# A two-part mixing network behind a linear recurrence: the whole first half in one written order, the token product on three column parts of the array, values and states stored head by head

## The chip, the cores and the metric

The kernel runs on one core of one Trainium2 chip. The metric is the device time of one execution in microseconds (us). The engines are TensorE (PE, with its weight loads PEld), VectorE (DVE), ScalarE (ACT), GpSimd (POOL) and SyncE (SP), whose queue issues nearly all transfers.

## What is computed

Four batches, eight heads, 768 positions, head size 48, so 384 channels. All arrays are float32 to the reference, but the weights arrive in a wider format and are unpacked on the chip.

```python
for t in range(S):                       # gated complex recurrence per head
    S_re, S_im = (ar*S_re - ai*S_im + k v^T, ar*S_im + ai*S_re)
    y[t] = q[t] . S_re
x = y as (batch, position, channel)
# first mixture
h = x^T @ U @ V                          # rank 32, over the positions
u = x + h^T
x = u + relu(u @ w_ch1) @ w_ch2          # 384 -> 1536 -> 384
# second mixture
theta = x @ w_theta
zr, zi = x*cos(theta), x*sin(theta)
u = x + w_tok_r @ zr + w_tok_i @ zi      # 768 x 768 over the positions
out = u + relu(u @ w_ch)
```

## The kernel before

**Attention.** The recurrence is computed in 24 chunks of 128 positions (six to a batch). Two chunks make a pair: `load` brings its four rows, `ew` does some 30 elementwise operations on 128 x 768 elements on VectorE and ScalarE (square roots, an arctangent, two running scans, sine and cosine), and `gather` moves the results into `QK`, one 96 x 258 block a head, with five transfers for each half of it. Then `pe_steps` does a chunk on TensorE: `score` (line 453, 8 products of 128 columns), `mask` and `select` (ScalarE copies the scores out, GpSimd zeroes the upper triangle), `ktr` (line 469, 8 transposes of k) and `kn_` (ScalarE copies them out), `xst` (line 492, 8 products for the new state), `add` (VectorE), `yt` (line 521, the output, two heads side by side on two 64-column halves of the array), `ycp`, `ytr` (line 535, transposed back) and a copy into `xs`. The values `vt` and states `a_st` are stored in pairs of heads with 48 zeros between the two, so that a product can take 96 or 64 columns from a head with zeros at the right place. `gx` (line 546) adds the chunk's share of x^T U with U repeated three times (96 columns of weights, 384 moving columns).

**First mixture.** `g_steps` splits x^T U into a high and a low part and multiplies by V (`hx`, line 576). `mlp_steps` then goes through three blocks of 256 positions a batch, each in six units: `f_unit` (line 711, 18 matmuls of 256 columns; ScalarE and VectorE copy the result out as `rh` and `rl`) and `c_unit` (line 736, 12 matmuls of 384 columns). `prologue` transposes x (line 682) for each block.

**Weights.** `unpack` turns each wide weight into a high and a low part with one load, one or two ScalarE and five VectorE operations: 22 jobs for the first mixture and U, V in the first phase, 16 for the second mixture, whose results partly go out to `tokd` in DRAM.

**What sets the order.** `startup` lists the steps of the first two batches' attention, of the jobs for the first mixture and of batch 0's `mlp_steps`. `ranks` gives each a rank (its longest path to the end, shifted by the table `LEAD`), `schedule` walks through time with a cost for every step (`COST`, `HOP`) and places the ready step with the lowest rank. `fixed` issues the steps in that order and ties VectorE, ScalarE and GpSimd to it (`HELD`). TensorE and the transfers are not tied; neither is anything of batches 2 and 3 (`attention`), of `mains` for batches 1 to 3 and of the 16 later jobs. Those are ordered by the compiler's list scheduler from the priorities of the lanes (`a2`, `a3`, `w3`, `moe`, `evac`).

**Second mixture.** `front` (projection, sine and cosine) and `mix` (the 768 x 768 product, line 971, and the channel product, line 987) run after that, ordered by the list scheduler.

Of the kernel before, what the change touches and what calls it, by code (L numbers as in the profile page):

```python
# [56 lines left out]
PLANNED = 2  # L57
# [30 lines left out]
def schedule(steps, rank, bias, hop=HOP, window=400):  # L88
# [20 lines left out]
    while ready:  # L109
        cand, low = [], 1e18  # L110
        for n in ready:
# [3 lines left out]
            if new:  # L115
                free = [x for x in frees[new[0][0]] if x is not None]
                if not free:
# [27 lines left out]
        at[e], end[n] = en, en + hop[e]  # L145
# [14 lines left out]

def ranks(steps, names, lead, hop=HOP):
# [4 lines left out]
    for n, nm in enumerate(names):  # L166
        if nm == "m0":
# [10 lines left out]
    for n, nm in enumerate(names):  # L178
        k = cnt[nm] = cnt.get(nm, -1) + 1
        r0, dr = lead.get(nm, (0, 0))  # L180
# [8 lines left out]
def attn_moe_kernel(tc, pk, qn, kn, v, are, aim, U, V, w1, w2, wth, wtr, wti, wch, out):  # L189
# [14 lines left out]
    ctx = ExitStack()  # L204
    const = ctx.enter_context(tc.tile_pool(name="const", bufs=1))
# [10 lines left out]
    stg = [xf[:, PLANNED * NC * C + i * 1536:PLANNED * NC * C + (i + 1) * 1536] for i in range(3)]  # L216
# [29 lines left out]
    vt_fs = [ac.tile([128, NP * 3 * D + 16], F32, name=f"vt{i}") for i in range(2)]  # L246
    vts = [t[:, 0:NP * 3 * D].rearrange("p (r z e) -> p r z e", z=3, e=D) for t in vt_fs]
    for t in vt_fs:
        G_.memset(t, 0.0)
    carry = ac.tile([128, NJ, 1], F32, name="carry")  # L250
    a_fs = [ac.tile([96, NP * 3 * D + 16], F32, name=f"a_st{i}") for i in range(2)]
    a_sts = [t[:, 0:NP * 3 * D].rearrange("p (r z e) -> p r z e", z=3, e=D) for t in a_fs]
    for t in a_fs:
        G_.memset(t, 0.0)
# [6 lines left out]
    wa = wp.tile([128, KF * C], F32, tag="w", name="wa")  # L261
    wb = wp.tile([128, KF * C], F32, tag="w", name="wb")
    e_store = dict(key="E", lo=er[:, 0:5], hi=er[:, 5:])

    w_store = dict(key="W", **{n: t[:, 0:5 * NR].rearrange("p (z n) -> p z n", z=5) for n, t in (("lo", wa), ("hi", wb))})
# [935 lines left out]
```

## Time and profile before

| | us |
|---|---|
| median of 3 runs | 877.26 (877.17 to 877.9) |
| the profiled execution | 877.16 |
| its span, first to last instruction | 875.4 |
| busy: PE / DVE / ACT / POOL | 757.8 / 524.9 / 453.3 / 124.3 |
| first matmul of the first mixture (line 711) | starts at 142.0 |
| last attention output leaves, last `hx` | about 495 |
| first matmul of the second token product (line 971) | starts at 642.4 |

The profile is read from the top: the slices tell where TensorE is full and at which granted clock, the windows give the busy time of each engine in a stretch, the waits name who held whom, and the chain of waits tells which of these ended last.

### The profile page before, as it was taken

How to read it: one execution, taken by the hardware profiler on the slowest of the kernel's cores; microseconds unless marked ns; L12 is line 12 of the kernel's file. 1: busy time of each engine (PE TensorE's matmuls, PEld its weight loads, DVE VectorE, ACT ScalarE, POOL GpSimd, SP SyncE). 2: the span in 40 equal slices, each digit the busy share in tenths (PEclk: the TensorE clock that was granted, in tenths of full speed). 3: DMA queues.
4: the chain of work that ended last, by engine and by line, in shares of the span. 5: the costliest groups of instructions: out<-in, count | busy, mean ns of one | idle time of the engine just before them, and what ended most of it. 6: DMA issues, size and time to landing. Idle time of an engine off the chain costs nothing.

```text
span 875.4 us, 13800 instructions
## 1 busy us (share of the span) xinstructions
PE 757.8 (87%) x5338; PEld 717.1 (82%) x5338; DVE 524.9 (60%) x787; ACT 453.3 (52%) x772; POOL 124.3 (14%) x144
## 2 busy tenths in 40 slices
PE   0085588798989698989999999899999999999996
PEld 0075367686978698979999999899999999999996
DVE  6958988978819578668151587893244335253321
ACT  6965876757726976784433253444155345253300
POOL 1011010200000002010101000000064234133200
PEclk9995867999998799999999999999999999999999
DMA  9264463552332443540331137620060000000001
GB/s 259 75 177 122 115 184 82 161 165 75 91 91 55 118 119 82 128 113 19 95 87 27 55 128 266 212 99 1 1 218 1 28 28 27 1 28 28 28 28 31
DMA packets 105657, 79.78 MB, mean 91 GB/s; under 512 B 32912, under 2 KB 97424, under 8 KB 105584
## 3 DMA queue, kind: packets, MB, share of 16 engines
q1 hardware_dynamic: 105184, 78.62, 32.2%
q8 instruction: 44, 0.72, 0.3%
q10 hardware_dynamic: 400, 0.20, 0.1%
q14 instruction: 29, 0.24, 0.1%
HBM read 50.33 MB, written 9.44 MB: 68 GB/s over the span
## 4 chain that ended last, share of the span: by engine, by line
PE 59%; DVE 15%; ACT 10%; DMA 8%; issue 3%; SPq 3%; POOL 0%; DVEq 0%; ACTq 0%; POOLq 0%
PE h L711 10%; PE c L736 9%; PE h L971 9%; PE c L971 9%; PE m L920 4%; PE m L987 4%; DVE er L337 4%; PE m L453 4%; PE m L521 4%; DMA er<-in_pk_dram 2%; ACT er L334 2%; DVE er L340 2%; PE m L492 2%; DMA tok1l<-tl 2%; ACT L334 2%
## 5 line engine op out<-in xcount | busy, mean ns | idle before, releaser
L711 PE MATMUL h<-uh,w1h 128*128 128x256 f32 x432 | 126.8, 294 | 3.1 <-DVE rl L721 2.1
L711 PE MATMUL h<-ul,w1h 128*128 128x256 f32 x432 | 125.0, 289 | 1.4 <-DVE ul L692 1.4
L711 PE MATMUL h<-uh,w1l 128*128 128x256 f32 x432 | 124.3, 288 | 0.0
L463 POOL TENSOR_SCALAR_AFFINE_SELECT pt<-pt 128x512 f32<-128x512 f32 x48 | 45.8, 962 | 425.7 <-ACT pt L459 411.2
L337 DVE TENSOR_TENSOR er<-er 128x768 f32<-128x768 f32 (+1 forms) x99 | 101.9, 1054 | 4.0 <-ACT er L334 2.0
L736 PE MATMUL c<-w2h,rl 128*128 128x384 f32 x288 | 100.1, 348 | 4.1 <-DVE rl L721 4.0
L736 PE MATMUL c<-w2h,rh 128*128 128x384 f32 x288 | 95.6, 349 | 6.7 <-ACT rh L716 3.0
L736 PE MATMUL c<-w2l,rh 128*128 128x384 f32 x288 | 97.8, 342 | 1.2 <-DVE w2l L311 1.1
L721 DVE SCALAR_TENSOR_TENSOR rl<-h,rh 128x512 fp32r<-128x512 f32 x72 | 49.3, 685 | 78.8 <-ACT rh L716 78.8
L711 PEld LDWEIGHTS h<-uh,w1h 128*128 128x128 f32 x432 | 83.5, 193 | 6.1 <-DVE rl L721 2.7
L711 PEld LDWEIGHTS h<-ul,w1h 128*128 128x128 f32 x432 | 83.6, 193 | 1.9 <-DVE ul L692 1.6
L711 PEld LDWEIGHTS h<-uh,w1l 128*128 128x128 f32 x432 | 83.5, 193 | 0.4 <-issue 0.2
L334 ACT ACTIVATE er<-er 128x768 f32<-128x768 f32 x88 | 74.0, 845 | 16.0 <-DVE er L337 12.4
L716 ACT ACTIVATE rh<-h 128x512 fp32r<-128x512 f32 x72 | 42.8, 596 | 67.4 <-PE h L711 59.5
L453 PE MATMUL m<-QK 96*128 96x128 f32 x384 | 60.0, 303 | 10.9 <-DMA QK<-wa 8.8
L453 PEld LDWEIGHTS m<-QK 96*128 96x128 f32 x384 | 53.5, 211 | 15.3 <-issue 10.5
L340 DVE SCALAR_TENSOR_TENSOR er<-er 128x768 f32<-128x768 f32 x55 | 52.8, 966 | 20.2 <-ACT er L334 11.6
L469 PE MATMUL m<-ident,QK 96*128 96x96 f32 x160 | 22.8, 261 | 46.0 <-DMA QK<-er 44.3
L736 PEld LDWEIGHTS c<-w2h,rh 128*128 128x128 f32 x288 | 52.8, 190 | 9.5 <-ACT rh L716 3.9
L736 PEld LDWEIGHTS c<-w2h,rl 128*128 128x128 f32 x288 | 54.6, 190 | 6.5 <-DVE rl L721 6.0
L469 PEld LDWEIGHTS m<-ident,QK 96*128 96x128 f32 x160 | 18.2, 150 | 49.6 <-issue 48.6
L736 PEld LDWEIGHTS c<-w2l,rh 128*128 128x128 f32 x288 | 54.3, 189 | 2.3 <-DVE w2l L311 1.8
(209 smaller groups left out, 1741.3 us busy)
## 6 DMA issues: line engine op xcount, KB each, us to landing
er<-in_pk_dram SPq DMA_DIRECT2D x88, 192.0 KB, 3.7
QK<-er SPq DMA_DIRECT2D x88, 145.1 KB, 3.4
x<-in_moe_w_ch_dram SPq DMA_DIRECT2D x9, 512.0 KB, 4.4
vt<-in_v_dram SPq DMA_DIRECT2D x48, 96.0 KB, 2.7
x<-in_moe_w_ch_dram SPq DMA_DIRECT2D x12, 384.0 KB, 3.4
st<-in_moe_w_tok_i_dram SPq DMA_DIRECT2D x6, 768.0 KB, 5.6
st<-in_moe_w_tok_r_dram SPq DMA_DIRECT2D x6, 768.0 KB, 4.2
out_dram<-x SPq DMA_DIRECT2D x23, 192.0 KB, 2.3
```

The source lines that it names most:

```text
L334: do("A", size, r, w, lambda e: A_.activation(out=out, in_=in_, func=func, **kw), tab)
L337: do("V", size, r, w, lambda e: V_.tensor_tensor(out=out, in0=in0, in1=in1, op=op))
L340: do("V", size, r, w, lambda e: V_.scalar_tensor_tensor(out=out, in0=in0, scalar=scalar, in1=in1, op0=op0, op1=op1))
L453: PE.matmul(ps[:, hh * T:(hh + 1) * T], lhsT=st["QK"][:, h, 1, 0:T], rhs=st["QK"][:, h, 0, 0:T], start=True, stop=True)
L463: G_.affine_select(out=pt, in_=pt, pattern=[[0, 4], [1, T]], compare_op=ALU.is_ge, fill=0.0, base=0, channel_multiplier=-1)
L469: PE.transpose(ps[:, hh * 96:(hh + 1) * 96], st["QK"][:, 4 * i + hh, 1, 0:T], ident[0:96, 0:96])
L521: PE.matmul(st["y"][64 * z:64 * z + 64, r * T:(r + 1) * T], lhsT=wide(old_w if k else vt_w, h), rhs=st["QK"][:, h, 0, 0:T] if k else st[f" ...
L711: PE.matmul(ps[:, f, :], lhsT=a[:, k, fs], rhs=u[:, k, :], start=(k == 0 and i == 0), stop=(k == NJ - 1 and i == 2))
L716: A_.activation(out=rh, in_=rts[n, p], func=AF.Relu)
L721: V_.scalar_tensor_tensor(out=rl, in0=ps, scalar=0.0, in1=r32(rh), op0=ALU.max, op1=ALU.subtract)
L736: PE.matmul(chs[n, t][:, 0:C], lhsT=r[:, f, t * T:(t + 1) * T], rhs=w[:, k, :], start=(k == 0 and i == 0), stop=(k == KF - 1 and i == 2))
L971: PE.matmul(ps[k][:, 0:C], lhsT=z[:, 2 * part + o, k * 128:(k + 1) * 128], rhs=w[:, s, ts], start=(s == 0 and part == 0 and j == 0), stop= ...
```

## The change

- `PLANNED` goes from 2 to 4: attention of all four batches and all four `mlp_steps` become steps of the plan, and so do the final flags, the reopening of the memory for the second mixture and its 16 weight jobs (`reopen`, `later`, `mix2_jobs`). `HELD` now ties TensorE and SyncE too. `attention` and `mains` go. Keys `fo` and `co` keep the units of all batches in one sequence; the table `LEAD` is new throughout.
- `gx` of batches 1 to 3 uses U once (32 columns) in three products of 128 moving columns on three 32-column parts of the array. The result lies in three blocks of 32 partitions, so `down` copies it out and `side` sends it through DRAM and back, three transfers each way.
- `vt` and `a_st` hold the heads one behind another without zeros. `xst` has 48 moving columns instead of 96; `yt` takes 64 columns, of which 16 belong to the next head and are not read later. The values need one transfer a chunk instead of two.
- `n2` (a rounding of 128 x 768 elements) may go to VectorE as well as ScalarE.

```diff
-    'l0': (17.6, 55.3), 'e0': (1.2, 0.1), 'p0': (-49.1, -22.6), 'u': (-11.1, 38.3), 'x0': (283.2, 62.0),
+    'l0': (-560.6, 1239.0), 'e0': (-3421.5, 1361.7), 'p0': (-1222.3, -173.9), 'u': (1269.9, -523.9),
...
-PLANNED = 2
+PLANNED = 4
...
-                    d = (1.05 if tab else 1.25) * size
+                    d = (1.05 if tab else 1.1) * size
...
-        at[e], end[n] = en, en + hop[e]
+        at[e], end[n] = en, en + (steps[n][5] if e == "D" and steps[n][5] else hop[e])
...
-    vt_fs = [ac.tile([128, NP * 3 * D + 16], F32, name=f"vt{i}") for i in range(2)]
+    vt_fs = [ac.tile([128, C + 16], F32, name=f"vt{i}") for i in range(2)]
...
-            for z in range(2):
-                nc.sync.dma_start(out=vt[:, :, 2 * z, :], in_=v[b, z::2, c * T:(c + 1) * T, :].rearrange("r s e -> s r e"))
+            nc.sync.dma_start(out=vt, in_=v[b, :, c * T:(c + 1) * T, :].rearrange("h s e -> s h e"))
...
-        act(AF.Identity, n2, Bt, bias=b_magic, r=K("B"), w=K("n"), size=N + 100)
+        do(EL, (N + 100) / 2, K("B"), K("n"), lambda e: V_.tensor_scalar(
+            out=n2, in0=Bt, scalar1=MAGIC, scalar2=None, op0=ALU.add) if e == "V" else
+            A_.activation(out=n2, in_=Bt, func=AF.Identity, bias=b_magic))
...
-                for r in range(NP):
-                    for z in range(2):
-                        h = 2 * r + z
-                        PE.matmul(ps[0:96, r * 96:(r + 1) * 96], lhsT=st["kn"][:, h, :],
-                                  rhs=vw(h), start=(z == 0), stop=(z == 1))
+                for h in range(H):
+                    PE.matmul(ps[0:96, h * D:(h + 1) * D], lhsT=st["kn"][:, h, :], rhs=vt_w[:, h * D:(h + 1) * D],
+                              start=True, stop=True)
...
+                for j in range(NJ):
+                    PE.matmul(gps["ps"][j * R:(j + 1) * R, 0:128], lhsT=u4[:, c, 0:R], rhs=xs[b][:, c, j * 128:(j + 1) * 128],
+                              start=(c == 0), stop=(c == NC - 1))
...
+        def down(e):
+            gps["t"] = t = ap.tile([128, H * 2 * D], F32, tag="kn", name="gt")
+            A_.copy(out=t[0:NJ * R, 0:128], in_=gps["ps"][0:NJ * R, 0:128])
+
+        def side(e):
+
+            t = gps["t"]
+            gps["ps"] = t[:, 128:128 + C]
+            gd = gdp.tile([R, NJ, 128], F32, tag="gd", name="gd")
+            for j in range(NJ):
+                nc.sync.dma_start(out=gd[:, j, :], in_=t[j * R:(j + 1) * R, 0:128])
+            for y in range(3):
+                nc.sync.dma_start(out=gps["ps"][y * R:(y + 1) * R, :], in_=gd.rearrange("r j c -> r (j c)"))
...
-    HELD = ('DVE', 'Activation', 'Pool')
+    HELD = ('DVE', 'Activation', 'Pool', 'PE', 'SP')
...
-        ops = mlp_steps(0)
-        steps.extend(ops)
-        names.extend("m0" if o[1] == "P" else "mv" for o in ops)
+        for b in range(PLANNED):
+            ops = mlp_steps(b)
+            steps.extend(ops)
+            names.extend(MAIN[b] if o[1] == "P" else f"mv{b or ''}" for o in ops)
...
+        for n, ops in enumerate(mix2_jobs()):
+            job(f"t{n}", ops)
```

How the order moves, at two places on TensorE. The first is the passage from batch 0's mixture to batch 1's: `up` is a prologue's transpose, `QK`, `kn`, `pt`, `yT` belong to an attention chunk, `h` and `c` are the mixture's two products. Before:

```order
L469 MATMUL m<-ident,QK 128x96 x3
L682 MATMUL up<-ident,x 128x128 x6
L492 MATMUL m<-vt_106,kn 96x96 x4
L521 MATMUL m<-pt_2263,vt_106 64x128 x4
L521 MATMUL m<-pt_2271,vt_106 64x128 x4
L492 MATMUL m<-vt_106,kn 96x96 x4
L535 MATMUL m<-ident,yT 128x128 x4
L711 MATMUL h<-uh,w1h 128x256
```

The same passage in the change (line 507 is the old 469, 491 the old 453, 528 the old 492, 557 the old 521, 571 the old 535, 741 the old 682):

```order
L795 MATMUL c<-w2l,rh 128x384
L507 MATMUL m<-ident,QK 128x96 x8
L491 MATMUL m<-QK 128x128 x8
L528 MATMUL m<-vt_108,kn 96x48 x8
L557 MATMUL m<-pt_2361,vt_108 64x128 x4
L557 MATMUL m<-pt_2343,vt_108 64x128 x4
L741 MATMUL up<-ident,x 128x128 x4
L571 MATMUL m<-ident,yT 128x128 x4
L491 MATMUL m<-QK 128x128 x8
L507 MATMUL m<-ident,QK 128x96 x8
```

Before, the chunk's scores stand further up, with mixture products between, and only its second half stands here. Now one whole chunk and the scores of the next stand one right behind the other, with no mixture product among them.

The second place is the last token product of batch 1 (`gps`) and what follows it. Before:

```order
L711 MATMUL h<-uh,w1h 128x256
L711 MATMUL h<-uh,w1l 128x256
L711 MATMUL h<-ul,w1h 128x256
L535 MATMUL m<-ident,yT 128x128 x4
L546 MATMUL gps<-x,u_132 96x384
L576 MATMUL m<-g_1960,v_133 128x384 x6
```

In the change:

```order
L770 MATMUL h<-uh,w1h 128x256
L770 MATMUL h<-uh,w1l 128x256
L770 MATMUL h<-ul,w1h 128x256
L588 MATMUL gps<-x,u_134 32x128 x3
L795 MATMUL c<-w2h,rh 128x384
L795 MATMUL c<-w2h,rl 128x384
L795 MATMUL c<-w2l,rh 128x384
```

Before, `hx` (line 576) stands right behind the token product. Now the token product has three parts, and mixture products stand between it and `hx` (line 635 now).

## Rows read from the trace of the kernel before

**Rows 1.** Windows: length, busy PE, PEld, DVE, ACT, POOL, granted clock, DMA share, GB/s.

```profile
0.00:45.00 45.00, 0.73 (x4) 0.77 (x5) 36.26 (x50) 36.58 (x49) 3.34 (x24) 1.00 0.66 164
45.00:142.00 97.00, 65.52 (x443) 53.01 (x442) 78.15 (x113) 67.16 (x110) 11.93 (x12) 0.73 0.54 140
142.00:495.00 353.00, 323.86 (x2595) 300.30 (x2596) 229.05 (x326) 207.49 (x349) 33.92 (x36) 0.96 0.35 92
495.00:643.00 148.00, 142.97 (x988) 139.53 (x987) 93.12 (x145) 56.64 (x91) 5.01 (x6) 1.00 0.38 128
643.00:876.00 233.00, 224.72 (x1315) 223.51 (x1313) 88.30 (x156) 85.47 (x174) 70.08 (x67) 0.99 0.10 32
```

**Rows 2.** The page's 40 slices: PE busy tenths and granted clock.

```profile
PE   0085588798989698989999999899999999999996
...
PEclk9995867999998799999999999999999999999999
```

**Rows 3.** Waits from 142 to 495 us: engine, line, releaser, total us, times, longest.

```profile
PE m L492 <- ACT kn L422: 8.5, 2, 6.9
...
DVE rl L721 <- ACT rh L716: 49.7, 15, 6.3
...
ACT yT L531 <- PE m L521: 31.8, 10, 5.5
...
SPq L307 <- PE m L521: 59.4, 10, 21.0
```

**Rows 4.** Timeline of PE and ACT near 299 us: start, us, operation.

```profile
299.16 1.60 PE L492 MATMUL m<-vt,kn 128*96 128x96 f32 x8 [6.86 <-ACT kn L422]
...
296.61 1.28 ACT L334 ACT_TABLE_LOAD   x1
297.90 0.84 ACT L334 ACTIVATE er<-er 128x768 f32<-128x768 f32 x1
298.65 0.46 ACT L422 COPY kn<-m 128x384 f32<-128x384 f32 x1
```

**Rows 5.** Window from batch 1's `hx` to its first mixture product.

```profile
264.00:305.00 41.00, 32.24 (x210) 31.20 (x211) 31.00 (x41) 33.25 (x48) 1.27 (x2) 0.80 0.33 88
```

**Rows 6.** Chain of waits: one unit of each mixture product, one chunk's scores.

```profile
141.96 3.35 PE h L711 x18
...
180.22 1.79 PE m L453 x16
...
626.04 2.11 PE c L736 x12
628.15 2.13 PE h L711 x18
```

**Rows 7.** Timeline of PE: token product and transposes of k (345), state and output (351).

```profile
345.26 0.81 PE L546 MATMUL gps<-x,u 128*96 128x384 f32 x2
345.90 0.50 PE L469 MATMUL m<-ident,QK 96*128 96x96 f32 x4
346.18 0.37 PE L711 MATMUL h<-ul,w1h 128*128 128x256 f32 x1
...
350.63 1.52 PE L492 MATMUL m<-vt,kn 128*96 128x96 f32 x16
352.08 0.44 PE L521 MATMUL m<-pt,vt 128*64 128x128 f32 x4
...
353.67 0.39 PE L521 MATMUL m<-QK,a_st 96*64 96x128 f32 x4
353.99 1.16 PE L453 MATMUL m<-QK 96*128 96x128 f32 x8
```

**Rows 8.** Timeline of PE: the mixture's eighth block begins.

```profile
493.83 0.28 PE L711 MATMUL h<-uh,w1h 128*128 128x256 f32 x1
```

**Rows 9.** Waits of PE from 45 to 142 us.

```profile
PE m L521 <- POOL pt L463: 6.7, 4, 2.2
...
PE m L535 <- ACT yT L531: 4.2, 4, 1.8
```

**Rows 10.** DMA issues: times, KB each, median us to landing; ScalarE's table loads.

```profile
QK<-er SPq DMA_DIRECT2D x88, 16.1 KB, 2.0
...
tok1h<-th SPq DMA_DIRECT2D x6, 384.0 KB, 4.9
...
L334 ACT ACT_TABLE_LOAD x31 | 39.8, 1283 | 0.9 <-DMA QK<-er 0.4
```

More of the change, by code (lines that the diff above doesn't have):

```diff
@@ L116, in schedule @@
                 free = [x for x in frees[new[0][0]] if x is not None]
-                if not free:
+                if len(free) < 1 + (new[0][0] == "ps" and len(new[0]) > 2):
                     continue
@@ L158, in schedule, with batch_of @@
     return sorted(out)
+MAIN = [f"m{b}" for b in range(PLANNED)]
+def batch_of(name):
+    per = {"l": NQ, "e": NQ, "p": NC, "x": NC, "g": 1}.get(name[0])
+    return int(name[1:]) // per if per and name[1:].isdigit() else 0
 def ranks(steps, names, lead, hop=HOP):
@@ L204, in attn_moe_kernel @@
     ctx = ExitStack()
+    gdp = ctx.enter_context(tc.tile_pool(name="gd", bufs=2, space=bass.MemoryType.DRAM))
     const = ctx.enter_context(tc.tile_pool(name="const", bufs=1))
@@ L215, in attn_moe_kernel @@
     xf = xall.rearrange("p b c d -> p (b c d)")
[L216 removed]
+    stg = [xf[:, STAGED * NC * C + i * 1536:STAGED * NC * C + (i + 1) * 1536] for i in range(3)]
     ident = const.tile([128, 128], F32, name="ident")
@@ L277, in attn_moe_kernel, with stages @@
         G_.memset(st["rows"][8][:, :, 0:1], 0.0)
+    def stages(b, c):
+        i = ((b - STAGED) * NC + c) * C
+        return sorted({("s0", "h0", "h1")[j // 1536] for j in (i, i + C - 1)}) if b >= STAGED else []
     EL = 'AV'
@@ L359, in ew @@
             out=flat(4), data0=flat(8), data1=d1.rearrange("p j c t -> p (j c t)"), initial=0.0, op0=ALU.mult, op1=ALU.add))
-        do("A", 6, K("A"), [("pc", pr)], lambda e: A_.copy(out=pcf[:, pr], in_=rows[4][:, :, T]))
+        do("A", 6, K("A"), [("pcf", pr)], lambda e: A_.copy(out=pcf[:, pr], in_=rows[4][:, :, T]))
         act(AF.Abs_reciprocal_sqrt, Dt, P2, "R", r=K("A"), w=K("D"))
@@ L502, in add @@
                 else:
-                    V_.tensor_tensor(out=nw, in0=psx(), in1=old[:, :, 0::2, :], op=ALU.add)
+                    V_.tensor_tensor(out=nw, in0=psx(), in1=hs(old), op=ALU.add)
             m = bank()
@@ L779, in run, with flags @@
             f(engs[0])
-    def attention(b):
-        gps = {}
-        for pr in range(b * NQ, (b + 1) * NQ):
-            run(load(pr, e_store))
-            run(ew(pr, e_store))
-            for g in (2 * pr, 2 * pr + 1):
-                a, m = pe_steps(g, gps)
-                run(a + m)
-        run(g_steps(b, gps))
+    env = {}
+    def flags(e):
+        fr = const.tile([128, 4], F32, name="fr")
+        V_.tensor_reduce(out=fr[:, 0:1], in_=flg, axis=mybir.AxisListType.X, op=ALU.max)
+        V_.tensor_reduce(out=fr[:, 1:2], in_=pcf.rearrange("p g j c -> p (g j c)"), axis=mybir.AxisListType.X, op=ALU.min)
+        V_.tensor_scalar(out=fr[:, 0:1], in0=fr[:, 0:1], scalar1=0.0, scalar2=None, op0=ALU.is_gt)
+        V_.tensor_scalar(out=fr[:, 1:2], in0=fr[:, 1:2], scalar1=P2_MIN, scalar2=None, op0=ALU.is_le)
+        V_.tensor_tensor(out=fr[:, 2:3], in0=fr[:, 0:1], in1=fr[:, 1:2], op=ALU.max)
+        V_.memset(fr[:, 3:4], 1.0)
+        env["fr"] = fr
@@ new lines, in flag_sum, with reopen @@
+    def flag_sum(e):
+        psf = ps_m.tile([128, 512], F32, tag="m", name="m")
+        fr = env["fr"]
+        PE.matmul(psf[0:1, 0:1], lhsT=fr[:, 2:3], rhs=fr[:, 3:4], start=True, stop=True)
+        env["psf"] = psf
+    def reopen(e):
+        V_.tensor_copy(out=fl_i, in_=env["psf"][0:1, 0:1])
+        at.close()
+        p2 = ctx.enter_context(tc.tile_pool(name="p2", bufs=1, reuse_waits="tile"))
+        dr = ctx.enter_context(tc.tile_pool(name="dr", bufs=1, space=bass.MemoryType.DRAM))
+        jb = ExitStack()
+        env.update(jb=jb, jp=jb.enter_context(tc.tile_pool(name="jb", bufs=2, reuse_waits="tile")),
+                   tok=[p2.tile([128, NC, S], F32R, name=f"tok0{y}") for y in "hl"],
+                   tokd=[dr.tile([128, NC, S], F32, name=f"tok1{y}") for y in "hl"],
+                   **{n: p2.tile([128, NJ, C], F32R, name=n) for n in ("wthh", "wthl", "wchh", "wchl")})
@@ L797, in job @@
             names.extend([name] * len(ops))
-        for b in range(PLANNED):
+        for b in range(B):
             gps = {}
@@ L888, in attn_moe_kernel @@
+    tok, tokd, wthh, wthl, wchh, wchl = [env[n] for n in ("tok", "tokd", "wthh", "wthl", "wchh", "wchl")]
+    env["jb"].close()
+    qp = ctx.enter_context(tc.tile_pool(name="q", bufs=2, reuse_waits="tile"))
     with lane("p2"):
```

179 lines of the change are left out of this document (88 added, 91 removed), and 42 rows, old and new, of the table LEAD.

## The prediction

> **What bounds the kernel now.** I read the windows first, in five stretches [rows 1]. TensorE is full from 643 us on (224.7 of 233 us) and nearly so from 495 (143 of 148), at a granted clock of 1.00 or just under. Nothing in the change touches the work after 643. From 142 to 495 TensorE is idle for 353 - 323.9 = 29.1 us, and its clock is 0.96 on the mean; the slices show where [rows 2]: the clock stands at 0.7 to 0.8 in places, first in the start and again near 280 us. Before 142 us VectorE (36.3 of 45, then 78.2 of 97 us) and ScalarE (36.6, 67.2) set the pace, and TensorE does little, at a clock of 0.73.
>
> How much of 142 to 495 is work? The chain of waits shows a unit of the first product, 18 matmuls, in 2.13 us and one of the second, 12 matmuls, in 2.11 [rows 6]. Exactly seven of the twelve blocks start in this stretch: the first matmul of the first block is at 141.96 [rows 6], that of the eighth at 493.83 [rows 8]. A block has six units of each, so 7 x 6 x 4.24 = 178.1 us. Eighteen attention chunks lie here as well. One costs, by starts at full clock: scores 1.79 us [rows 6]; transposes of k, 4 in 0.28, so 0.56; state 352.08 - 350.63 = 1.45; output 353.99 - 352.08 = 1.91; transposes back about 0.28; token product 345.90 - 345.26 = 0.64 [rows 7]. That is 6.63, times 18 is 119.3, less 3 x (0.56 + 1.45) for chunks that pass no state on and 3 x 0.95 for chunks that receive none: 110.4. Block transposes (42 at 0.07) and 18 products of V (0.32 at most, half a token product) add 8.7. The sum is 297 us, so 353 - 297 = 56 us are lost: 29 idle, the rest to the lower clock and to refilling after waits.
>
> Who holds TensorE? The waits name many small ones and one large [rows 3]: the state product waited 8.5 us for ScalarE's copy of k, 6.86 of it at once near 299 us. The timeline of that place is plain: ScalarE had an activation and its 1.28 us table load ahead of the copy [rows 4]. The passage around it, from batch 1's `hx` to its first block, takes 41 us with TensorE busy for 32 and the clock at 0.80 [rows 5]. In the other direction VectorE waits 49.7 us for ScalarE's `rh`, ScalarE 31.8 us for outputs of TensorE, and the transfer queue stands 59.4 us behind the load of values [rows 3]. No engine is full in this stretch (VectorE 229 of 353, ScalarE 207 [rows 1]). The order, more than any engine, is the limit.
>
> **The change part by part.**
>
> *The common order.* It removes no work. It can give back at most the 56 us, plus some 5 us idle after 495. Three things speak for a return: the blocks are spread so that batch 1's attention and batch 0's last block go together, the passage of [rows 5] holds about 16 us of TensorE work by the new order in place of 24, and TensorE, ScalarE and the transfer queue follow one plan, whose loads of values stand where their buffer is meant to be free. Against it: in the new order the products of a chunk often stand directly behind each other. I take half, 28 us, since neither end has a row that decides; the ends are 0 and 56. The 5 us after 495 I leave.
>
> *The start.* By counting rows ahead of the first mixture product, VectorE has seven more weight jobs and less attention there; at the mean durations that comes to some 4 us more of 114 [rows 1]. Its idle time there is 27 us. I leave 142 us as it is and keep 10 us either way.
>
> *Token product.* Eighteen of 24 change. Now 0.64 us [rows 7]. A part has 128 moving columns, as the output product has. There two heads on two halves of the array take about 0.22 us for their four instructions: the eight groups of a chunk start from 352.08 to 353.67, a little more apart after the first, and the next product starts at 353.99. Eight times 0.22 of 1.91 leaves 0.15 us for the borders, 0.10 of it on leaving [rows 7]. If three parts run side by side as the two do, a token product takes 0.22 + 0.15 = 0.37 us and saves 0.27, in all 4.9 us. If they run one after another it takes 3 x 0.22 + 0.15 = 0.81, a loss of 3.1 us. Without any loss at the borders it saves 7.6. The 0.15 us is what speaks against this part. The Trainium skill (TensorEngine Tiling (Array Packing), Key Properties) says that a change of tiling mode, not of tile alone, drains TensorE; it gives no figure, and the trace agrees in that 0.10 us shows on leaving.
>
> *The way through DRAM.* Per batch 1 to 3: a copy of 128 columns, three transfers out, three back. Small transfers land in 2.0 us, larger ones to DRAM in 4.9 [rows 10]. Twice 2.0 to 4.9 us plus the issues is 5 to 12 us. In the new order 9 to 12 us of TensorE work stand between the last token product and `hx`, so I cost it at nothing. If that cover is gone it costs up to 3 us a time, 9 us in all; only batch 1 is pressed, since batches 2 and 3 start their blocks over 50 us of TensorE work later.
>
> *State product.* 16 instructions in 1.45 us [rows 7], 0.091 each, with half the moving columns now. The weights, 96 columns, stay. The nearest row is the transposes of k, whose weights have 128 columns and which start every 0.07 us [rows 7]. At 0.07 the product takes 1.12 us: 0.33 saved, for 15 chunks after 142 us 5.0 us. The ends are no gain and half the time, 10.9 us. The Trainium skill (TensorE: Matmul & The Clock Gate, LDWEIGHTS) gives a weight load as its columns over 1.2, here an estimate of 80 ns, so 2.6 us saved and a time 2 us later; the trace does not agree for the transposes, where it would want 107 ns and 70 are seen.
>
> *The rest, at nothing:* one transfer of values a chunk less (hidden, the queue waits there anyway); four table loads more on ScalarE by the new order, 4 x 1.28 = 5.1 us [rows 10] on an engine with 146 us idle in 353; `n2` on VectorE or ScalarE.
>
> *Sum,* against the profiled execution's 877.16 us (the median of three runs is 877.26): 877.2 - 28 - 4.9 - 5.0 = **839 us**. The 10 us either way in the start, 28 in the order and 3 to 8 in the products set the bounds of this case: 820 to 857.
>
> **The rivals.**
>
> *All stalls go.* The plan covers everything TensorE needs. Then 56 us come back with 10 of the products, 811 us. For it: no engine is full. Against: an order in a plan with fixed costs never fits every duration. Chance 0.20.
>
> *Stalls only move.* VectorE and ScalarE still hand over to each other at the same rate, so that the blocks come no earlier than 142 + 353; the products' savings fall into idle time, and the 5 us after 495 and a few more come back: 868 us, range 857 to 875.5. For it: VectorE's waits for `rh` are not a matter of TensorE's order. Against: the passage [rows 5]. Chance 0.14.
>
> *Short distances, slower.* Between a chunk's first score product and its output the new order leaves 2.4 us of TensorE work (median), before 5.8. Where these distances were as short, in the first chunks, TensorE waited 1.7 us each time for GpSimd's masking (6.7 in 4) and 1.05 for the copy of the output (4.2 in 4) [rows 9]. TensorE now cannot pass a waiting product. Two masks and one copy a chunk make 4.45 us, in 18 chunks 80 us, 919 us at worst. It decides the sign from 38.2 / 4.45, or nine chunks on; with twelve it is 839 + 53 = 892 us. Against it: in the first chunks there was no mixture work to put between, now there is. Chance 0.13.
>
> *The change doesn't do what it says:* the three parts run one after another. Then 8 us of the sum go, 847 us, inside the forecast's own bounds.
>
> **How the numbers follow.** A measurement of this kernel can tell about 0.2%, 1.8 us, from no change. The forecast has a chance of 0.50, the rival without stalls 0.20, moved stalls 0.14, short distances 0.13; 0.03 is left for within 0.2%. Faster by more: 0.50 + 0.20 + 0.14 = 0.84; the same 0.03; slower 0.13. The range runs from 808, just below the rival without stalls, to 874, the end of moved stalls; it leaves out the slower rival and some 0.06 below.
>
> **What would show it.** Right: the first block still near 142 us, the eighth near 455, the second token product from about 603 us, idle of TensorE between first block and `hx` of the last batch near 15 us, the token product's six instructions within 0.4 us, the state product's 16 near 1.1. Wrong: idle time in that stretch of 30 us or more, with GpSimd's mask, the copies of k or the return from DRAM as releasers, or a clock below 0.95 there; a state product that still takes 1.4 us; or the start moved by more than 10 us, which I have no row for.

## The result and the profile after

The changed kernel takes **838.3 us** (median of 4 runs, 836.17 to 845.32) against 877.58 beside it: a ratio of 0.9564, 95% interval 0.9507 to 0.9621. A second set of five runs gave 841.59 (ratio 0.9577, 0.9554 to 0.9601). The forecast was 839 us in a range of 808 to 874. The profiled execution took 838.51 us, span 836.8, against 877.16 and 875.4 before.

The total is right; several terms of the sum are not, and their misses cancel. Where the time went is read from four stretches that hold the same blocks in both kernels: to the first block of the first mixture, from there to the eighth, to the first product of the second mixture, and to the end. The last three, for the kernel before (columns as in [rows 1]):

```profile
141.90:493.80 351.90, 322.70 (x2586) 299.14 (x2587) 228.83 (x326) 207.58 (x349) 33.92 (x36) 0.96 0.36 92
493.80:642.40 148.60, 143.57 (x993) 140.13 (x992) 92.91 (x145) 56.64 (x91) 4.41 (x5) 1.00 0.37 126
642.40:875.40 233.00, 225.32 (x1319) 224.11 (x1317) 88.82 (x158) 85.47 (x174) 70.68 (x68) 0.99 0.10 33
```

The same for the change and, last, the passage that answers to [rows 5], from batch 1's `hx` to its first block:

```profile
142.10:460.20 318.10, 307.47 (x2664) 288.67 (x2664) 239.14 (x326) 205.79 (x341) 33.28 (x36) 0.99 0.40 103
460.20:600.60 140.40, 137.83 (x967) 136.43 (x966) 89.42 (x132) 52.01 (x81) 0.98 (x2) 1.00 0.37 129
600.60:836.80 236.20, 228.64 (x1339) 227.33 (x1337) 89.67 (x162) 89.24 (x183) 73.42 (x72) 0.99 0.09 30
...
264.00:283.50 19.50, 17.63 (x169) 16.38 (x168) 18.51 (x28) 16.27 (x25) 4.77 (x4) 1.00 0.62 154
```

The start did not move (141.90 to 142.10). The long stretch shrank by 33.8 us, the next by 8.2, the last grew by 3.2: 38.8, which is the difference of the spans but for 0.2.

The 33.8 can be taken apart. TensorE's idle time fell from 351.9 - 322.7 = 29.2 to 318.1 - 307.5 = 10.6, so 18.6. The mean granted clock rose from 0.96 to 0.99; at the lower of its two levels (1.2 GHz, the other 2.4) work takes about twice as long: the products of the first block start 0.21 us apart at 142 us, those of the eighth 0.12. In the kernel before, three whole stretches stand at the lower level:

```profile
171.40:178.20 6.80, 5.89 (x25) 5.53 (x24) 5.77 (x11) 1.53 (x4) 0.00 (x0) 0.50 0.50 137
260.20:270.50 10.30, 7.79 (x28) 6.71 (x29) 10.23 (x16) 5.99 (x9) 0.00 (x0) 0.50 0.00 0
294.30:304.50 10.20, 5.03 (x32) 4.29 (x32) 3.75 (x5) 10.13 (x16) 0.64 (x1) 0.50 0.30 82
```

TensorE is busy for 18.7 of these 27.3 us, so some 9.4 us are lost to the clock; the other 8.6 are idle time, which is counted already. The change has no such stretch; only the low one of the start reaches 3.8 us behind its first block, for 2.2 before, which costs it 0.8. That leaves some 8.5 us. The token product gave about 3 (below). Together that is 30 of the 33.8; the other 4 are assigned to nothing. So **with 18.6 us of idle time some 8.5 us of lost clock went too**, a little under half a microsecond for each. That the one brought the other is argued, not tested; the third stretch sets in while TensorE waits its 6.86 us for the copy of k [rows 4]. The page's slices of the clock show it too: the dip to 0.7 that [rows 2] have near 280 us is gone, only those before 150 us stay:

```profile
PEclk9996757999999999999999999999999999999998
```

What TensorE still waits for in that stretch (all rows over 0.3 us; engine, line, releaser, total us, times, longest), and three waits of other queues that answer to [rows 3]:

```profile
PE m L557 <- POOL pt L501: 3.0, 7, 0.7
PE m L557 <- DMA vt<-in_v_dram: 2.8, 1, 2.8
PE m L491 <- DMA QK<-er: 2.3, 4, 1.4
PE m L571 <- ACT yT L567: 0.9, 2, 0.6
PE h L770 <- DVE ul L751: 0.5, 1, 0.5
PE m L557 <- ACT pt L497: 0.5, 2, 0.3
PE m L635 <- DVE x L640: 0.4, 1, 0.4
...
DVE rl L780 <- ACT rh L775: 33.5, 16, 6.6
...
ACT yT L567 <- PE m L557: 19.4, 11, 3.4
...
SPq L343 <- PE m L557: 27.5, 7, 6.4
```

The 8.5 us for the copy of k, 6.9 of them at once, are gone. So are the mixture's own waits. In the kernel before they were (same stretch, the five largest rows of `h` and `c`):

```profile
PE c L736 <- DVE x L741: 2.9, 1, 2.9
PE c L736 <- ACT rh L716: 2.4, 2, 1.4
...
PE h L711 <- DVE rl L721: 2.1, 2, 1.8
...
PE c L736 <- DVE rl L721: 1.5, 2, 1.3
...
PE c L736 <- DVE w2l L311: 1.1, 1, 1.1
```

With two smaller rows that is 11.7 us in ten waits: 6.0 of it for the ReLU's output `rh` and its remainder `rl`, the rest for a sum into `x`, the inputs `ul` and parts of the weights. Now a single 0.5 is left. VectorE's wait for `rh` is 33.5 for 49.7, ScalarE's for the output 19.4 for 31.8, the load of values 27.5 for 59.4.

The two products that changed, on TensorE's timeline: a token product between mixture products, and a state product with the output behind it (start, us, operation).

```profile
253.66 0.28 PE L770 MATMUL h<-ul,w1h 128*128 128x256 f32 x1
253.87 0.42 PE L588 MATMUL gps<-x,u 128*32 128x128 f32 x6
254.22 0.44 PE L795 MATMUL c<-w2h,rh 128*128 128x384 f32 x1
254.50 0.34 PE L795 MATMUL c<-w2h,rl 128*128 128x384 f32 x1
...
281.02 1.56 PE L528 MATMUL m<-vt,kn 128*96 128x48 f32 x16
282.51 0.44 PE L557 MATMUL m<-pt,vt 128*64 128x128 f32 x4
```

The token product's six instructions take 0.35 us to the next start, as forecast. The state product's sixteen take 282.51 - 281.02 = 1.49 us, not 1.1; before it was 1.45 [rows 7]. Each of these times has 0.18 us in it from the start of the last of the sixteen to the start of the output behind.

### The profile page after: what moved, and what is told of

It is laid out like the page before. It is cut to its first block, busy times and chain, and to the rows that moved or that the text cites. A ratio compares the mean times of both kernels' runs of the same rounds, so it can differ in the third digit from the quotient of the medians.

```text
span 836.8 us, 13921 instructions
## 1 busy us (share of the span) xinstructions
PE 740.8 (89%) x5410; PEld 707.6 (85%) x5410; DVE 538.9 (64%) x800; ACT 452.0 (54%) x766; POOL 119.5 (14%) x144
## 4 chain that ended last, share of the span: by engine, by line
PE 65%; DVE 12%; DMA 8%; ACT 7%; SPq 4%; issue 3%; POOL 1%; DVEq 0%; ACTq 0%; POOLq 0%
PE h L770 12%; PE c L795 12%; PE h L1056 9%; PE c L1056 9%; PE m L1072 4%; PE m L1005 4%; PE m L491 4%; PE m L557 4%; PE m L528 3%; DVE er L373 2%; ACT er L370 2%; DMA er<-in_pk_dram 2%; DMA QK<-er 2%; DMA st<-in_moe_w_tok_r_dram 1%; DMA st<-in_moe_w_tok_i_dram 1%
## 5 line engine op out<-in xcount | busy, mean ns | idle before, releaser
L770 PE MATMUL h<-uh,w1h 128*128 128x256 f32 x432 | 124.9, 289 | 0.8 <-DVE ul L751 0.5
L770 PE MATMUL h<-ul,w1h 128*128 128x256 f32 x432 | 122.5, 284 | 0.0
L770 PE MATMUL h<-uh,w1l 128*128 128x256 f32 x432 | 122.4, 283 | 0.0
L373 DVE TENSOR_TENSOR er<-er 128x768 f32<-128x768 f32 (+1 forms) x99 | 104.1, 1065 | 11.8 <-ACT er L370 4.4
L795 PE MATMUL c<-w2h,rh 128*128 128x384 f32 x288 | 101.3, 352 | 0.0
L795 PE MATMUL c<-w2h,rl 128*128 128x384 f32 x288 | 97.5, 338 | 1.9 <-DVE rl L780 1.9
L501 POOL TENSOR_SCALAR_AFFINE_SELECT pt<-pt 128x512 f32<-128x512 f32 x48 | 43.7, 916 | 384.7 <-ACT pt L497 383.5
L491 PE MATMUL m<-QK 96*128 96x128 f32 x384 | 56.8, 301 | 9.5 <-issue 7.0
L507 PE MATMUL m<-ident,QK 96*128 96x96 f32 x160 | 21.1, 272 | 46.7 <-DMA QK<-er 46.7
```

Of the source, the lines that this page charges most:

```text
L373: do("V", size, r, w, lambda e: V_.tensor_tensor(out=out, in0=in0, in1=in1, op=op))
L491: PE.matmul(ps[:, hh * T:(hh + 1) * T], lhsT=st["QK"][:, h, 1, 0:T], rhs=st["QK"][:, h, 0, 0:T], start=True, stop=True)
L501: G_.affine_select(out=pt, in_=pt, pattern=[[0, 4], [1, T]], compare_op=ALU.is_ge, fill=0.0, base=0, channel_multiplier=-1)
L507: PE.transpose(ps[:, hh * 96:(hh + 1) * 96], st["QK"][:, 4 * i + hh, 1, 0:T], ident[0:96, 0:96])
L770: PE.matmul(ps[:, f, :], lhsT=a[:, k, fs], rhs=u[:, k, :], start=(k == 0 and i == 0), stop=(k == NJ - 1 and i == 2))
L795: PE.matmul(chs[n, t][:, 0:C], lhsT=r[:, f, t * T:(t + 1) * T], rhs=w[:, k, :], start=(k == 0 and i == 0), stop=(k == KF - 1 and i == 2))
```

## The experiments

All ratios are against the kernel before, run on the same chip in the same job; medians in us. Each experiment from the changed kernel is its edit alone, unless it says otherwise.

**The change again**, nothing edited, as the yardstick.

> The changed kernel once more, as the mark for the three beside it. Both theories: 838.3 us as before, 836 to 845; the state product's 16 instructions in 1.45 to 1.5 us, a token product's six in about 0.35.

Measured: 841.59 (837.27 to 845.49, five runs), ratio 0.9577 (0.9554 to 0.9601). Its profiled execution (span 843.8) starts the first block at 145.83 and needs 321.4 us to the eighth, where the first had 142.10 and 318.1. So some 4 us of start and 3 us of the stretch are spread between runs of one program, and half a per cent between medians is at the edge of what can be told.

**State product with 96 moving columns**, each head's surplus overwritten by the next head's product.

```diff
-    vt_fs = [ac.tile([128, C + 16], F32, name=f"vt{i}") for i in range(2)]
+    vt_fs = [ac.tile([128, C + 48], F32, name=f"vt{i}") for i in range(2)]
...
-                    PE.matmul(ps[0:96, h * D:(h + 1) * D], lhsT=st["kn"][:, h, :], rhs=vt_w[:, h * D:(h + 1) * D],
+                    PE.matmul(ps[0:96, h * D:(h + 2) * D], lhsT=st["kn"][:, h, :], rhs=vt_w[:, h * D:(h + 2) * D],
```

> The changed kernel with 96 moving columns in the state product again (the second half of each is overwritten by the next head's product); order and everything else as in the changed kernel. Theory that the weights pace it: the 16 instructions still take 1.45 to 1.5 us and the time is that of e1_again within 2 us. Rival that the moving columns pace it: 16 x 0.02 to 0.04 us more a chunk, 1.8 to 2.1 us, and the time 6 to 10 us longer.

Measured: 839.63 (836.49 to 843.53), ratio 0.9561 (0.9541 to 0.9580). Twice the columns cost nothing that the time shows. On the timeline:

```profile
285.07 1.60 PE L528 MATMUL m<-vt,kn 128*96 128x96 f32 x16
286.60 0.44 PE L557 MATMUL m<-pt,vt 128*64 128x128 f32 x4
```

That is 1.53 us with 96 columns; the change again has the same chunk at 1.48 with 48. By the single starts in both traces the sixteen follow each other at 0.085 us from the second one on, with 48 columns as with 96. The moving columns do not pace this product. What both share is the weight load of 96 columns for each instruction; that this load is what paces it is not shown, since no run changed it.

**Token product in one piece**: 96 x 384 for all batches as in the kernel before, the copy out of the accumulator kept, the way through DRAM gone; same steps in the same order.

```diff
-            if b == 0:
+            if True:
...
-            A_.copy(out=t[0:NJ * R, 0:128], in_=gps["ps"][0:NJ * R, 0:128])
+            A_.copy(out=t[0:NJ * R, 128:128 + C], in_=gps["ps"][0:NJ * R, 0:C])
...
-            gd = gdp.tile([R, NJ, 128], F32, tag="gd", name="gd")
-            for j in range(NJ):
-                nc.sync.dma_start(out=gd[:, j, :], in_=t[j * R:(j + 1) * R, 0:128])
-            for y in range(3):
-                nc.sync.dma_start(out=gps["ps"][y * R:(y + 1) * R, :], in_=gd.rearrange("r j c -> r (j c)"))
```

> The changed kernel with the token product of batches 1 to 3 as one product of 96 weight and 384 moving columns and no way through DRAM; the list of steps and its order stay. Theory of the prediction: a token product takes 0.64 us instead of about 0.44, 18 x 0.2 = 3.6 us more, 841 to 843. Rival that the way through DRAM holds up the products of V and costs more than the parts save: 833 to 837, with fewer waits between the last token product and the products of V.

Measured: 842.24 (839.17 to 845.62), ratio 0.9615 (0.9589 to 0.9641); first to eighth block 319.7 us, between the change's own 318.1 and 321.4. The medians lean towards a small loss, the stretch towards none. The timeline is sharper. The place of the fence above, in this kernel:

```profile
253.50 0.28 PE L765 MATMUL h<-ul,w1h 128*128 128x256 f32 x1
253.62 0.81 PE L583 MATMUL gps<-x,u 128*96 128x384 f32 x2
253.97 0.63 PE L790 MATMUL c<-w2h,rh 128*128 128x384 f32 x1
254.44 0.34 PE L790 MATMUL c<-w2h,rl 128*128 128x384 f32 x1
```

From the last `h` to the second `c` it takes 0.94 us in one piece and 254.50 - 253.66 = 0.84 in three parts. Without the steps of the `h` (0.12) and of the `c` (0.18) that is 0.64 against 0.54: **0.10 saved, not 0.27**. Of the 0.54, 0.09 lie ahead of the parts (they start 0.21 after the `h`, a plain step is 0.12) and 0.10 behind (the second `c` comes 0.28 after the first, a plain step is 0.18). Where the output stands in front and a mixture product behind (318 us), the rows give 1.16 in one piece and 0.89 in parts, so 0.27 saved; where two token products stand together, 0.99 in one piece and 0.56 in parts to the next start. Added up by the starts at all eighteen places in the two traces, where 0 to 0.29 are saved, it is 3.1 us.

**The three parts on the same 32 columns of the array**, one behind the other, all else as in the change (the copy and the transfers out take their rows from there).

```diff
-                    PE.matmul(gps["ps"][j * R:(j + 1) * R, 0:128], lhsT=u4[:, c, 0:R], rhs=xs[b][:, c, j * 128:(j + 1) * 128],
-                              start=(c == 0), stop=(c == NC - 1))
+                    PE.matmul(gps["ps"][0:R, j * 128:(j + 1) * 128], lhsT=u4[:, c, 0:R], rhs=xs[b][:, c, j * 128:(j + 1) * 128],
+                              start=(c == 0 and j == 0), stop=(c == NC - 1 and j == NJ - 1))
...
```

> The changed kernel with the three parts of the token product on the same 32-column part of the array, one behind the other in the same partitions; way through DRAM and order as in the changed kernel. Theory that the parts run side by side in the changed kernel: six instructions take 0.64 to 0.8 us instead of 0.35, 18 x 0.3 to 0.45 = 5 to 8 us more, 843 to 846. Rival that they were not side by side: 0.35 us and 838 as before.

Measured: 843.48 (842.44 to 848.02), ratio 0.9620 (0.9604 to 0.9636); first to eighth block 326.0 us, TensorE busy for 318.0 of them.

```profile
258.94 0.28 PE L770 MATMUL h<-ul,w1h 128*128 128x256 f32 x1
259.15 0.84 PE L588 MATMUL gps<-x,u 128*32 128x128 f32 x6
259.92 0.44 PE L795 MATMUL c<-w2h,rh 128*128 128x384 f32 x1
```

Six instructions take 0.77 us to the next start here and 0.35 in the change, 0.42 more; times 18 is 7.6, and the stretch is 4.6 to 7.9 longer. So the three parts do run side by side, and the rival in which they don't is out. It is the timeline that shows it: the medians, 843.48 and 841.59 for the change again beside it, are only 1.9 us apart.

**TensorE free, SyncE tied** (the four-batch plan stays).

```diff
-    HELD = ('DVE', 'Activation', 'Pool', 'PE', 'SP')
+    HELD = ('DVE', 'Activation', 'Pool', 'SP')
```

> The changed kernel with the tie on TensorE taken away (SyncE, VectorE, ScalarE and GpSimd still tied): the list scheduler may place TensorE's products otherwise. Theory that the one order of TensorE gives back the stalls: idle of TensorE between first block and eighth rises from 11 us towards 20 to 30, 848 to 858 us. Rival that the plan's order of VectorE, ScalarE and GpSimd alone does it: 838 within 3 us.

Measured: 870.71 (866.84 to 873.53), ratio 0.9948 (0.9921 to 0.9975). Of 38 us only some 5 are left, and the time is 13 us beyond the theory's 858, though its 20 to 30 us of idle time came (25.2). **TensorE's fixed order carries about 32 us**: 26 in the long stretch (344.2 for 318.1 us) and up to 6 in the start (the first block comes at 147.9 for 142.1). The passage of [rows 5] is nevertheless short here too (17 us). The time goes in small waits all over the long stretch, and most of them are the mixture's:

```profile
148.00:492.00 344.00, 318.78 (x2663) 295.45 (x2664) 238.81 (x325) 204.87 (x340) 32.54 (x36) 0.97 0.36 95
...
PE c L795 <- ACT rh L775: 7.8, 6, 2.0
...
PE c L795 <- DVE rl L780: 1.9, 4, 0.5
PE h L770 <- DVE rl L780: 1.8, 2, 1.5
```

With two smaller rows `h` and `c` wait 12.7 us, where the change has 0.5; idle is 25.2 and the clock 0.97. The state product's wait for the copy of k is gone here as well, without the tie.

**SyncE free, TensorE tied.**

```diff
-    HELD = ('DVE', 'Activation', 'Pool', 'PE', 'SP')
+    HELD = ('DVE', 'Activation', 'Pool', 'PE')
```

> The changed kernel with the tie on SyncE's transfers taken away, TensorE still tied. Theory: the loads move but the order of the products stays, 838 to 845 us. Rival that the order of the transfers is what removed the stalls: 850 us and more, with the transfer queue waiting 50 us or more on the loads of values as before.

Measured: 838.30 (833.19 to 840.94), ratio 0.9558 (0.9513 to 0.9602). The tie of the transfer queue brings nothing that can be told from the 3 us between the two sets of runs of the change.

**Both free.**

> The changed kernel with the ties on TensorE and SyncE both taken away, as in the kernel before, but all four batches still planned. Theory: the sum of the two single losses, 848 to 865 us. Rival that only planning all batches for VectorE and ScalarE counts: 838 within 3 us.

Measured: a median of 881.93 in four runs from 866.93 to 888.22, profiled at a clock of 0.931; no interval came of it. Nothing is concluded from it.

**The kernel before with TensorE and SyncE tied** (its two-batch plan, its table, its layout).

```diff
-    HELD = ('DVE', 'Activation', 'Pool')
+    HELD = ('DVE', 'Activation', 'Pool', 'PE', 'SP')
```

> The kernel before with TensorE and SyncE tied in its own plan of two batches; the rest is ordered by the list scheduler as before. Theory that the planning of all batches brings the gain: 877 us, 870 to 885. Rival that the tie brings it: 845 to 860.

Measured: 864.41 (862.45 to 868.48), ratio 0.9869 (0.9847 to 0.9891), between the ranges of the two. The tie alone brings 12 us, the new plan without TensorE's tie 5 (with the change's token product in it), both together 38. Some 21 us exist only where the new plan *and* the tie come together. How much of them is due to better places, and how much to the tie now covering four batches where the old plan holds two, was not tried.

**Which half of TensorE's order?** Two kernels tie TensorE within one kind of work only. First the first mixture's steps alone (`MAIN` holds their names):

```diff
-                if i.engine in held:
+                if i.engine in held and (i.engine != mybir.EngineType.PE or env["mix"][sn[1]]):
...
+        env["mix"] = [n in MAIN for n in names]
```

> The changed kernel with TensorE tied to the fixed order only for the first mixture's own steps (prologue, f and c units, mixture sums and projections); the attention and token steps of TensorE are placed freely again, as with TensorE wholly free (870.7 us, against 838.3 for the change). Theory A: what the tie brings is that each attention product comes at its planned place, early enough for the chain behind it (scores, mask, y, next state); then this kernel keeps little of the 30 us: 855 to 872, with the stretch from the first f block to the eighth at 335 us or more. Rival B: what it brings is that units of the mixture stay whole and in sequence, so that no unit waits for the GELU of the one before; then 836 to 848 and a stretch near 320.

Measured: 873.64 (870.47 to 875.77), ratio 0.9969 (0.9951 to 0.9988); first to eighth block 346.8 us. Nothing is kept. (The kernel has no GELU; what rival B means is the ReLU of the mixture, whose output is `rh`.) Then all other steps alone (the same edit with `not env["mix"][sn[1]]`):

> The opposite half: TensorE tied for the attention, token and state steps, and free for the first mixture's steps. Theory A: most of the gain stays, 836 to 850, with the stretch from the first f block to the eighth at 318 to 330 us. Rival B: 855 to 872. If both halves land near 870, only the order between the two kinds of work matters (which product stands between which units), and neither half carries it alone.

Measured: 861.09 (855.89 to 870.74), ratio 0.9801 (0.9746 to 0.9857); first to eighth block 340.9 us. Each theory missed one of the two. Theory A asked for 836 to 850 here, and rival B for 836 to 848 with the mixture tied. Against TensorE wholly free (870.71) the mixture's own order brings nothing (3 us slower), that of the rest some 10 (its interval alone is 5 us either way), both together 32: the other 20 or so hang on the order *between* the two kinds. Nearly 6 of the 10 are an earlier first block (142.1 for 147.9, where two runs of the change differ by 4); in the long stretch the order of the rest gives back 3 of 26 us. The waits agree: tied in either half alone, the mixture's products wait for the ReLU again. With the mixture tied:

```profile
150.00:497.00 347.00, 322.29 (x2667) 301.01 (x2668) 240.07 (x327) 205.49 (x341) 30.98 (x36) 0.96 0.37 94
...
PE c L795 <- ACT rh L775: 4.8, 4, 2.0
PE c L795 <- DVE rl L780: 2.5, 4, 0.9
```

With two smaller rows `h` and `c` wait 9.3 us here.

With the rest tied:

```profile
142.00:483.00 341.00, 318.82 (x2664) 296.23 (x2664) 239.79 (x326) 205.87 (x340) 32.56 (x36) 0.97 0.37 96
...
PE c L795 <- ACT rh L775: 6.9, 6, 2.0
PE h L770 <- DVE rl L780: 1.5, 1, 1.5
```

With three smaller rows that is 10.6 us.

**The plan without its table**, both queues tied as in the change.

```diff
-LEAD = {
-    'l0': (-560.6, 1239.0), 'e0': (-3421.5, 1361.7), 'p0': (-1222.3, -173.9), 'u': (1269.9, -523.9),
...
+LEAD = {}
```

> The changed kernel with the table of priorities emptied, so that the steps are planned by the length of the chain behind each alone; TensorE and the issuing queue stay tied to that plan. The change swapped this table together with the tie, and the plan of before with the tie gave 864.4 (against 838.3 and 877.6). Theory: the gain is that of this one order, not of tying as such, so a plain order that is followed as strictly gives 860 to 890, by waits of TensorE for ScalarE, VectorE and GpSimd products that stand too close behind their makers (40 us or more idle from the first f block to the eighth, against 11 in the change). Rival: any common order does, 836 to 846.

Measured: 908.47 (905.48 to 912.49), ratio 1.0378 (1.0329 to 1.0427), beyond the theory's own 890. The first block comes earlier, at 130.05, and the eighth at 501.96:

```profile
130.00:502.00 372.00, 327.06 (x2665) 306.17 (x2666) 256.14 (x363) 211.57 (x353) 35.03 (x36) 0.92 0.36 95
502.00:670.00 168.00, 147.62 (x979) 143.53 (x978) 92.13 (x139) 53.43 (x85) 1.32 (x2) 0.96 0.33 120
...
PE h L738 <- DVE rl L748: 12.0, 4, 6.1
PE h L738 <- DVE ul L719: 11.4, 3, 8.1
PE c L763 <- DVE rl L748: 8.4, 2, 7.6
```

TensorE is idle for 45 us in the first stretch and 20 in the second, and the clock falls to 0.92 with it. The waits are single and long (up to 8.1 us), and VectorE is behind them. The theory had the place and the idle time right and the releasers wrong in part: it named ScalarE, VectorE and GpSimd, and some 35 of the 45 us are VectorE. The empty table reorders every engine, so it was not shown which engine's order does the harm. What it shows is that a common order as such can cost 33 us as well as bring 38: the gain depends on which order it is.

**The kernel before with values and states by heads**, nothing else of the change.

```diff
-    vt_fs = [ac.tile([128, NP * 3 * D + 16], F32, name=f"vt{i}") for i in range(2)]
+    vt_fs = [ac.tile([128, C + 16], F32, name=f"vt{i}") for i in range(2)]
...
-            for z in range(2):
-                nc.sync.dma_start(out=vt[:, :, 2 * z, :], in_=v[b, z::2, c * T:(c + 1) * T, :].rearrange("r s e -> s r e"))
+            nc.sync.dma_start(out=vt, in_=v[b, :, c * T:(c + 1) * T, :].rearrange("h s e -> s h e"))
...
-                for r in range(NP):
-                    for z in range(2):
-                        h = 2 * r + z
-                        PE.matmul(ps[0:96, r * 96:(r + 1) * 96], lhsT=st["kn"][:, h, :],
-                                  rhs=vw(h), start=(z == 0), stop=(z == 1))
+                for h in range(H):
+                    PE.matmul(ps[0:96, h * D:(h + 1) * D], lhsT=st["kn"][:, h, :], rhs=vt_w[:, h * D:(h + 1) * D],
+                              start=True, stop=True)
...
```

> The kernel before with values and states by heads (one product of 48 columns per head for the state, no zero columns, one load of the values for each chunk instead of two) and nothing else changed. Theory: the state product is paced by its weights of 96 columns at about 0.093 us each, so 16 products still take about 1.5 us (1.45 in the kernel before), and half as many rows for VectorE and half as many loads are hidden: 874 to 879, the kernel before's time. Rival, the prediction's own term: the narrower product and the shorter VectorE steps give 4 to 6 us, 870 to 873.

Measured: 876.17 (873.70 to 879.16, ten runs), ratio 1.0005 (0.9984 to 1.0025). The layout alone is worth nothing, with an end at 2 us either way. Its state product, and what follows:

```profile
347.67 1.48 PE L487 MATMUL m<-vt,kn 128*96 128x48 f32 x16
349.08 0.44 PE L516 MATMUL m<-pt,vt 128*64 128x128 f32 x4
```

That is 1.41 us, where the kernel before has 1.45 in its nearest chunk [rows 7].

The three stretches of the profiled executions side by side, in us:

```
                                     first block   to the eighth   to mixture 2   to the end
before                                     141.9           351.9          148.6        233.0
before, PE and SP tied                     136.9           348.0          148.7        233.2
before, by heads                           138.5           354.6          147.9        232.6
change                                     142.1           318.1          140.4        236.2
change again                               145.8           321.4          140.4        236.1
state product with 96 columns              143.2           322.2          140.4        236.0
token product in one piece                 141.9           319.7          140.2        235.7
parts on the same columns                  143.5           326.0          140.7        236.1
SyncE free                                 144.1           318.8          138.8        236.1
TensorE free                               147.9           344.2          141.3        234.8
TensorE tied, mixture only                 149.8           346.8          140.9        236.2
TensorE tied, all but the mixture          142.1           340.9          141.4        234.5
no table                                   130.1           371.9          167.9        235.7
```

Two things stand out. The 7 to 10 us less in the third column and the 1.5 to 3 more in the fourth come with the four-batch plan and its table, whether TensorE is tied or not. The second column is short only where TensorE is tied throughout and follows the new plan.

## Why the prediction was right, and where it was not

**Common order, -28, ends 0 and 56: right in place, and in size by luck.** The stretch gave 33.8, of which the token product has about 3, so the order gave some 30. TensorE free gives 32 us back in the whole time. The 28 was half of 56 with no row to decide it, and both parts were off: 29.2 us of idle time and 10.5 of clock make some 40 us lost, not 56, and three quarters came back, not half. The sum of 297 us of work was too low by some 12: without its idle time and its 1.9 us of clock the change's stretch still takes 305.6, where 297 - 3 would be 294. The rivals that all stalls go (811 us) and that they only move (868 us) are both answered: 10.6 us idle and a clock of 0.99 are left.

**Its reason was only half right.** The prediction leaned on one large stall, the passage of 41 us [rows 5]. That passage is 19.5 us now, as it said, but it is 17 in the kernel with TensorE free, which is 32 us slower. A passage that gets shorter proves nothing: work moves out of it and waits elsewhere. The large stall, the wait for the copy of k, went with the new plan of the other engines, and the kernel that has this plan without the tie is only 5 us ahead of the kernel before. What the tie removed was many small waits, those of the mixture's products first of all: 11.7 us before, 12.7 with TensorE free, 9.3 and 10.6 with either half tied, 0.5 in the change. For the ReLU's output and its remainder alone it is 6.0, 11.5, 9.0, 9.4 and none. That an attention product now stands where a unit used to wait is what the order shows at the places ahead of the prediction; that this and no other feature of the order matters was not tried.

**Start unchanged: right** (141.9 to 142.1), with some 4 us between two runs of one program.

**Token product, -4.9 at 0.27 each: too much, -3.1 by the starts.** The body was right: two token products together take 0.56, so the second adds 0.21 to the 0.35 of one, where 0.22 was taken. The borders failed: "0.15 for the borders" came from the output product. Between mixture products they are 0.09 in front and, behind, 0.35 - 0.21 = 0.14 up to the next start and 0.10 more on the product after it, 0.33 in all. So there 0.10 is saved, not 0.27. By the Trainium skill (TensorEngine Tiling (Array Packing), Key Properties) a change of tiling mode drains TensorE. These rows agree with it on the way in: the parts start 0.21 us after the `h`, where the product in one piece, which is not tiled, starts after 0.12. On the way out they can't separate it, for the product in one piece delays the `c` behind it as well.

**State product, -5.0: wrong, nothing.** The step that failed is the price "at 0.07", taken from the transposes of k as the nearest row. The product takes 1.49 us for 16 instructions with 48 columns, 1.53 with 96, and 1.45 in the kernel before: halving the moving columns changes it by less than the chunks differ. The stated end "no gain" was the value, and a product that still takes 1.4 us was one of the prediction's own signs of being wrong. The row was misread on both sides. Four transposes take 0.28 us to the next start [rows 7], but eight of them, in the same kernel, take 0.61:

```profile
329.47 0.83 PE L469 MATMUL m<-ident,QK 96*128 96x96 f32 x8
330.08 0.42 PE L736 MATMUL c<-w2h,rh 128*128 128x384 f32 x1
```

Four more add 0.33, so they are 0.083 apart and not 0.07: the product behind starts 0.03 after the last one, and 0.28 / 4 shares that short step out. The state product's 0.091 had its 0.18 up to the output in it; its own step was 0.085 already. So the two rows differ by next to nothing, and there was nothing to save. By the Trainium skill (TensorE: Matmul & The Clock Gate, LDWEIGHTS) a load goes by its columns, an estimate of 80 ns for 96. The state product's 85 ns are near it; the transposes' 83, with loads of 128 columns and an estimate of 107, are not. Why these are faster is open.

**The stretch after the eighth block, left alone: wrong by 5 us.** It lost 8.2 us, of which 3.2 came back behind, where 16 or so projection products of 0.18 each now stand; net 5.0, half of it less idle time of TensorE (5.0 before, 2.6 now); the other half is assigned to nothing. Every kernel with the four-batch plan and its table does this. This 5.0 is what hid the state product's miss: 30 + 3 + 0 + 5 against 28 + 4.9 + 5.0 + 0.

**The way through DRAM at nothing: right.** Its transfers land in 1.5 and 1.8 us in the median, and `hx` waits 0.4 us in that stretch, for VectorE.

**The slower rival, 892 us by short distances**, did not come in the change: GpSimd's mask holds TensorE 3.0 us in seven waits of at most 0.7, not 1.7 each. But a common order that loses is real: without the table it took 908 us, with VectorE and not the mask as its place. The price of 4.45 us a chunk was taken from the first chunks, which have no mixture work between; with it, a mask costs 0.4.

**"Wrong if idle is 30 or more, or the clock below 0.95"**: 10.6 and 0.99. The second token product and the eighth block came at 600.6 and 460.2, forecast 603 and 455.

## What to carry to other kernels

Tie TensorE to an order only together with a plan made for it: tie alone 12 us, plan alone 5, both 38, and a plain order tied as strictly was 33 us slower than the kernel before. Price idle time of TensorE with its clock: here 18.6 us of idle went together with some 8.5 us of clock. Before you narrow a product, find out whether its moving columns or its weights pace it: the instruction's time at two widths, side by side, says so, and a different product's row does not. Take the step of a product from its own starts: the time to the next row's start, divided by the count, has the border to another product in it.

## What the hardware showed that was not expected

- Float32 instructions with 96 weight columns, each with new weights, start 0.085 us apart with 48 moving columns and with 96.
- Three products on three 32-column parts of the array take 0.35 us where the same three on one part take 0.77; the borders to full-width products cost 0.33 us, more than the 0.21 that the three parts themselves add.
- A token product in one piece (2 instructions, 384 moving columns) shows 0.35 us to the next start, but the `c` behind it then needs 0.47 to its own successor instead of 0.18. The next row's start alone understates such a product by 0.29; the second row after it has to be read.
